# Running two feed-forward units' up halves before their down halves at the start of an attention + MLP kernel

## The chip, the cores and the metric

The kernel runs on one core of a Trainium2 chip. The metric is the device time of one execution, in microseconds; lower is better. Before the change it was 218.37 us, the median of 3 runs (217.48 to 218.43). A run that comes with a profile gives two numbers: its device time, and the span from the first to the last instruction in the trace, which is shorter. The two are never mixed in a subtraction below.

## The reference

Attention over chunks of 32 queries, each with 16 keys to its left, 8 to its right and 8 memory keys, then a normalisation and a two-layer MLP with a residual:

```python
for c in range(S // 32):                    # q, k, v: (4, 8, 768, 64)
    k_full = concat([mem_k, k[:, :, c*32-16 : c*32+40]])     # same for v
    a = softmax(q_c @ k_full.T / 8)
    out[:, :, c*32 : c*32+32] = a @ v_full
x  = out.transpose(0, 2, 1, 3).reshape(4, 768, 512)
xn = (x - mean) / sqrt(var + 1e-6) * g_ln
y  = x + relu(xn @ w_ch1) @ w_ch2           # 512 -> 2048 -> 512
```

## The kernel before

The work is cut into 24 tiles of 128 tokens (6 for each batch entry), and three tiles make a unit, so there are 8 units. Per tile: `scores` (8 matmuls into an `att` slot of PSUM, two exps on ScalarE), `values` (matmuls into the other `att` slot), `norm` (four VectorE instructions that read this slot and leave `xn`), `turn_x` (four transposes of `xn` into a slot, then a ScalarE copy to `xT`). Per unit: 16 `up` chunks (four matmuls of N=384, then a relu on VectorE or ScalarE in turn) and 12 `down` pieces (four matmuls of N=512). PSUM has two `att` slots and four `mm` slots, given out in turn. In the traces every engine takes its instructions in the order of the program; the relu at 40.60 us in the profile after, which stands behind a norm, is the case that matters most.

```python
att = [ps.tile([128, 2, 512], FP32, name=f"att{i}") for i in range(2)]
mm = [ps.tile([128, 512], FP32, name=f"mm{i}") for i in range(4)]
rT = [sb.tile([128, 384], FP16, name=f"rT{hc}") for hc in range(16)]   # one unit's relus
def stay_busy(n, p=None):                  # dummy matmuls on a tile of zeros
    p = slot("mm") if p is None else p
    for _ in range(n):
        nc.tensor.matmul(out=p, lhsT=busy[:, 0:128], rhs=busy, start=True, stop=True)
def clear_q(i, par):                       # zero half of the spread-out queries QZ[i]
    nc.vector.memset(QZ[i][64 - 64 * par : 128 - 64 * par, :, :, par, :], 0.0)
```

The head, cut to TensorE's dummies and VectorE's clears, and the start of unit 0:

```python
stay_busy(10)
clear_v(0, nc.vector, lambda: clear_q(0, 0)); clear_q(0, 1); clear_k(0)
mem_keys(); mem_cols(0)
stay_busy(4)
v_mem(0)                                   # memory rows of the values, by DMA
...                                        # turn keys and queries; stay_busy(3), stay_busy(4)
nc.tensor.matmul(out=banks[2], lhsT=ones32, rhs=g_one, start=True, stop=True)   # g to all rows
nc.vector.tensor_copy(out=g_row, in_=banks[2])
...                                        # tiles 0 to 2: scores, values, norm, turn_x, ups 0-3
for hc in range(4, 8): up(0, 2, hc)
for hc in range(8): up(0, 3, hc, 2)
...                                        # then, in the loop over units, for u == 0:
at(7, clear_q, 1, 0); at(9, clear_q, 1, 1); at(10, clear_k, 1)
at(15, kq_block, ...)                      # second half of batch 0's keys and queries
attend(((17, 19, 19, 22), (18, 21, 21, 24), (20, 23, 23, 26)), "att")   # unit 1's attention
```

`at(step, ...)` places work behind step `step` of a unit: steps 0 to 15 are its ups, the later ones its downs. The numbers of `attend` are the steps of scores, values, norm and turn_x of the three tiles that follow. So before the change, unit 1's attention is spread between unit 0's down pieces.

The softmax here doesn't subtract the row's maximum and nothing guards it: scores larger than these inputs give would overflow.

Of the kernel before, what the change touches and what calls it, by code (L numbers as in the profile page):

```python
# [15 lines left out]
def kernel(  # L16
# [29 lines left out]
    memv16 = sb.tile([72, B, H, HD], FP16, name="memv16")[64:72, :, :, :]  # L46
    memv32 = sb.tile([72, 512], FP32, name="memv32")[64:72, :]
# [12 lines left out]
    qraw = [sb.tile([128, 4096], FP16, name=f"qraw{i}") for i in range(2)]  # L60
    QT = kraw[1]
    k16 = [t[0:96, 0:4096].rearrange("p (h r d) -> p h r d", h=H, r=8) for t in kraw]
    q16 = [t[0:96, 0:4096].rearrange("p (h r d) -> p h r d", h=H, r=8) for t in qraw]
# [7 lines left out]
    rT = [sb.tile([128, 384], FP16, name=f"rT{hc}") for hc in range(16)]  # L71
    osb = [sb.tile([128, 512], FP32, name=f"osb{i}") for i in range(3)]
    total = [sb.tile([128, 1], FP32, name=f"total{i}") for i in range(3)]
    nmean = [sb.tile([128, 1], FP32, name=f"nmean{i}") for i in range(3)]
# [29 lines left out]
    def load_kq(b, which, lo=0, hi=96, h0=0, h1=H):  # L104

        dst, src = ((k16, k), (q16, q))[which]
        nc.gpsimd.dma_start(
            out=dst[b % 2][lo:hi, h0:h1, :, :],
            in_=dram(src, (b * H + h0) * HS + 512 * lo,
                     [[512, hi - lo], [HS, h1 - h0], [1, 512]]),  # L110
        )
# [22 lines left out]
    def v_mem(b):  # L134
        src = memv16[:, b, :, :]
        nc.sync.dma_start(
            out=V[b % 2][96:104, :, :, :],
            in_=bass.AP(tensor=src.tensor, offset=src.offset,
                        ap=[list(src.ap[0]), [0, NG], [1, H * HD]]),
        )  # L140
# [68 lines left out]
    def kq_block(b, j, g0, g1, kind, last=nc.scalar.copy):  # L209

        pk, pq = slot("att"), None
        if kind == "att":
            pq = slot("att")
            pq = [pq[:, i, :] for i in range(2)]
        else:
            pq = [slot("mm")[:, :] for i in range(2)]
        for i in range(2):
            turn_kq(as16(pk[:, i, :]), k16[b % 2], j + i, 96)
        for i in range(2):
            turn_kq(as16(pq[i]), q16[b % 2], j + i, 96)  # L220

        def keep(i):
            keep_k(as16(pk[:, i, :]), b, j + i, 96, g0 + 1 if g0 else 0, g1)
            for par in range(2):
                keep_q(last if i else nc.scalar.copy, as16(pq[i]), b, j + i, par, 96, g0, g1)

        keep(0)
        kept_later.append(lambda: keep(1))
# [11 lines left out]
    def load_tokens(b, which, t):  # L240
        dst, src = ((kraw[0], k), (qraw[0], q))[which]
        nc.gpsimd.dma_start(  # L242
            out=free(dst, 512 * t, [[64, H], [1, 64]]),
            in_=dram(src, b * H * HS + 128 * t * D, [[D, 128], [HS, H], [1, 64]]),
        )
# [7 lines left out]
    def cross_q(half, t0, t1):  # L253
        nc.sync.dma_start_transpose(
            out=free(QT, (24 * half + 4 * t0) * 64, [[64, 4 * (t1 - t0)], [1, 64]]),
            in_=qraw[0][64 * half : 64 * half + 64, 512 * t0 : 512 * t1],
        )
# [58 lines left out]
    def norm(t, xi):  # L316
        x, p = xs[xi], summed.pop(t)
        r, i = rec[t % 2], t % 3
        nc.vector.reciprocal(out=r, in_=free(p, 64, [[128, H]]))
        nc.vector.scalar_tensor_tensor(  # L320
            out=x.rearrange("p (h d) -> p h d", h=H),
            in0=free(p, 0, [[128, H], [1, 64]]), scalar=1.0,
            in1=free(r, 0, [[1, H], [0, 64]]),
            op0=ALU.mult, op1=ALU.mult, accum_out=total[i],
        )
        nc.vector.tensor_scalar(  # L326
            out=nmean[i], in0=total[i], scalar1=-1.0 / 512, scalar2=None, op0=ALU.mult,
        )
        nc.vector.scalar_tensor_tensor(  # L329
            out=xn[i], in0=x, scalar=nmean[i], in1=g_row, op0=ALU.add, op1=ALU.mult,  # L330
        )

    def root(t, xi):
        i = t % 3
        nc.scalar.activation(  # L335
            out=junk, in_=xs[xi], func=ACTF.Square, bias=nmean[i], accum_out=squares[i],
        )
        nc.gpsimd.tensor_scalar(  # L338
            out=veps[i], in0=squares[i], scalar1=1.0 / 512, scalar2=1e-6,
            op0=ALU.mult, op1=ALU.add,  # L340
        )
        nc.gpsimd.tensor_tensor(out=rstd[xi], in0=veps[i], in1=mhalf, op=ALU.pow)  # L342
# [27 lines left out]
    def up(u, n, hc, t0=0, on_act=False):  # L370
# [10 lines left out]
        o = rT[hc][:, lo:hi]  # L381
# [7 lines left out]
    def down(t, i, part):  # L389
# [3 lines left out]
        for hc in range(4 * part, 4 * part + 4):  # L393
            nc.tensor.matmul(  # L394
                out=p, lhsT=rT[hc][:, 128 * i : 128 * i + 128],
                rhs=w2c[hc // 4][:, hc % 4, :],
                start=(hc == 0), stop=(hc == 15),
            )
# [7 lines left out]
    def down_last(t, i):  # L406

        o = osb[t % 3]
        for lo, hi in ((0, 256), (256, 384), (384, 512)):
            p = slot("mm")[:, 0 : hi - lo]  # L410
            for hc in range(16):
                nc.tensor.matmul(  # L412
                    out=p, lhsT=rT[hc][:, 128 * i : 128 * i + 128],
                    rhs=w2c[hc // 4][:, hc % 4, lo:hi],
                    start=(hc == 0), stop=(hc == 15),
                )
# [17 lines left out]
    def clear_q(i, par):  # L434

        nc.vector.memset(QZ[i][64 - 64 * par : 128 - 64 * par, :, :, par, :], 0.0)  # L436

    def clear_v(i, eng, between=lambda: None):
# [3 lines left out]
        eng.memset(V[i][:, :, :, 64:HD], 1.0)  # L442
        between()
        for c, g in enumerate((0, NG - 1)):
            eng.tensor_copy(
                out=free(V[i][:, g, 0, 64:65], 0, [[HD, H]]),
                in_=free(counts[:, c : c + 1], 0, [[0, H]]),
            )
# [14 lines left out]
    nc.vector.memset(memv16[:, :, :, 64:HD], 1.0)  # L463
# [3 lines left out]
    for h in (0, 4):  # L467
        for which in range(2):
            load_kq(0, which, 0, CUT[which], h, h + 4)
    keep(counts[:, 0:1], counts[:, 0:1], 16, 0.0)  # L470
    keep(counts[:, 1:2], counts[:, 1:2], -80, 0.0)
    make_identity(nc, identity)
    nc.scalar.copy(out=memk16, in_=memk32)
    nc.scalar.copy(out=memv16[:, 0, :, 0:64], in_=memv32.rearrange("p (h d) -> p h d", h=H))
    stay_busy(10)
    clear_v(0, nc.vector, lambda: clear_q(0, 0))
    clear_q(0, 1)
    clear_k(0)
    mem_keys()
    mem_cols(0)  # L480
    stay_busy(4)
    v_mem(0)
    for g in range(6):
        load_v_group(0, g)
# [11 lines left out]
    for c in range(4):  # L496
        load_w1(c)
    for which in range(2):
        load_kq(0, which, CUT[which], 96)
    load_w2(0)  # L500
    load_w2(1)
    for g in range(6, 10):
        load_v_group(0, g)
    load_w2(2)
    for g in range(10, NG):
        load_v_group(0, g)
    load_w2(3)
# [10 lines left out]
    spare = att[(turn["att"] + 1) % 2][:, 0, :]  # L518
    for j in range(2):
        turn_kq(first_k[j], k16[0], j, CUT[0])  # L520
    for j in range(2):
        turn_kq(first_q[j], q16[0], j, CUT[1])
# [5 lines left out]
    for j in range(2, 4):  # L528
        turn_kq(first_k[j], k16[0], j, CUT[0])
# [3 lines left out]
    for j in range(2, 4):  # L533
        turn_kq(first_q[j], q16[0], j, CUT[1])
# [4 lines left out]
    nc.tensor.matmul(out=banks[2], lhsT=ones32, rhs=g_one, start=True, stop=True)  # L539
    nc.vector.tensor_copy(out=g_row, in_=banks[2])  # L540
# [22 lines left out]
    turn_x(0, 2, 2)  # L563
    for hc in range(4, 8):
        up(0, 2, hc)
    for hc in range(8):
        up(0, 3, hc, 2)
# [3 lines left out]
    for u, tiles in enumerate(units):  # L571
        n = len(tiles)
        following = units[u + 1] if u + 1 < len(units) else []
        plan = {}

# [3 lines left out]
        def attend(steps, kind="dma"):  # L579

            for i, (s0, s1, s2, s3) in enumerate(steps):
# [5 lines left out]
                at(min(s3 + 3, 27), root, t % 6, t % 9)  # L587
# [10 lines left out]

        if u == 0:
            at(7, clear_q, 1, 0)  # L600
            at(9, clear_q, 1, 1)
            at(10, clear_k, 1)
            at(23, clear_v, 1, nc.gpsimd)
            for j in (0, 2):
                at(15, kq_block, 0, j, 6, NG, "mm", nc.vector.tensor_copy if j else nc.scalar.copy)
                at(15, keep_rest)
            for t in range(3):
                at(19 + t, root, t, t)
            for h in (0, 4):
                for which in range(2):  # L610
                    at(15, load_kq, 1, which, 0, 96, h, h + 4)
            for g in range(6):
                at(23, load_v_group, 1, g)
            attend(((17, 19, 19, 22), (18, 21, 21, 24), (20, 23, 23, 26)), "att")
            at(26, mem_cols, 1)
            at(26, v_mem, 1)
        elif u == 1:
            for j in (0, 2):
                at(5 + 3 * j, kq_block, 1, j, 0, NG, "att")
                at(7 + 3 * j, keep_rest)  # L620
            for g in range(6, NG):
                at(0, load_v_group, 1, g)
            for t in range(6):
                for which in range(2):
                    at(14, load_tokens, 2, which, t)
            attend(((16, 19, 19, 22), (17, 19, 20, 23), (21, 23, 23, 26)), "att")
# [34 lines left out]
        for step in range(16 + 4 * n):  # L661
            if step < 16:
                if u or step > 7:
                    up(u, n, step)
            else:
                i, part = divmod(step - 16, 4)
                if u == 0:
                    i, part = (step - 16) % 3, (step - 16) // 3
                if following or i < n - 1:
                    down(tiles[i], i, part)  # L670
# [34 lines left out]
```

## Time and profile before

| | before |
|---|---|
| device time, median | 218.37 us |
| span of the profiled run | 216.0 us |
| TensorE busy | 210.2 us, 97% |
| VectorE / ScalarE busy | 118.6 / 99.7 us |
| VectorE stall of TensorE behind the head | one, 0.71 us at 28.44 us |

TensorE is the bound. The page of the profile adds one line that becomes important later: the clock that TensorE was granted, in 40 equal slices of the span, each digit in tenths of full speed.

```profile
PEclk9999999999999999999999999999999999999998
```

Two quantities are used in what follows. The first is the *lost time* of a TensorE instruction: the time from its predecessor's start to its own start, less the time that the predecessor takes in steady state (0.216 us for N=512, 0.1625 for N=384, 0.056 for N=128, all from unbroken stretches of this trace). It doesn't depend on the modelled ends of matmuls. The second is the start of the first exp, which marks the end of the head: 13.07 us before.

### The profile page before, as it was taken

Reading aid. Unit: us, or ns where it says so; the run is one execution under the profiler, and the core shown is the slowest. Engines: PE = TensorE matmul, PEld = TensorE weight load, DVE = VectorE, ACT = ScalarE, POOL = GpSimd, SP = SyncE. Lnnn points to the kernel's source line nnn. Section 1 sums busy time; section 2 is a strip of 40 time slices with the busy share of each in tenths; the row PEclk is TensorE's granted clock in tenths of the full one; section 3 lists DMA queues with packets and bytes.
Section 4 is the critical chain, followed back from the end, with each engine's and each line's share of the span. In section 5 each row is a group of like instructions: output and inputs, shape, how many; then the busy total and the mean of one; then the engine's idle time right before and its main releaser. Section 6 shows DMA issues by size and latency. Waiting matters only on the chain.

```text
span 216.0 us, 5059 instructions
## 1 busy us (share of the span) xinstructions
PE 210.2 (97%) x2011; PEld 129.8 (60%) x2011; DVE 118.6 (55%) x274; ACT 99.7 (46%) x206; POOL 104.4 (48%) x185
## 2 busy tenths in 40 slices
PE   7999989999999999999999999999999999999993
PEld 2557866557765577546754676456754675466562
DVE  6967675685737548524375349224484447634222
ACT  4478437855893677302653167103761275314100
POOL 7993245699996318974004998507145000400000
PEclk9999999999999999999999999999999999999998
DMA  5999999999999989996312999997674101330012
GB/s 78 182 150 207 209 208 181 200 206 226 148 140 172 102 135 146 151 146 171 48 27 80 142 186 148 138 156 103 176 150 132 49 3 24 91 108 0 0 49 100
DMA packets 87714, 27.37 MB, mean 127 GB/s; under 512 B 78297, under 2 KB 84185, under 8 KB 87642
## 3 DMA queue, kind: packets, MB, share of 16 engines
q0 software_dynamic: 62128, 14.38, 78.2%
q1 hardware_dynamic: 25562, 12.66, 28.2%
q8 instruction: 16, 0.26, 0.5%
q14 instruction: 8, 0.07, 0.1%
HBM read 28.84 MB, written 6.29 MB: 163 GB/s over the span
## 4 chain that ended last, share of the span: by engine, by line
PE 94%; DVE 3%; ACT 1%; issue 1%; ACTq 0%
PE mm L377 37%; PE mm L394 37%; PE att L289 5%; PE att L309 3%; PE mm L366 3%; PE att L179 2%; PE mm L412 2%; PE mm L179 1%; DVE QZ L436 1%; ACT AT L296 1%; PE att L352 1%; PE att L366 1%; DVE rT L385 1%; PE mm L539 0%; DVE xn L329 0%
## 5 line engine op out<-in xcount | busy, mean ns | idle before, releaser
L377 PE MATMUL mm<-xT,w1c 128*128 128x384 f16 (+2 forms) x560 | 89.0, 313 | 0.6 <-DVE rT L385 0.6
L394 PE MATMUL mm<-w2c,rT 128*128 128x512 f16 x368 | 84.4, 379 | 0.0
L377 PEld LDWEIGHTS <-w1c 128*128 128x128 f16 x560 | 58.8, 114 | 23.6 <-issue 1.0
L383 ACT ACTIVATE rT<-mm 128x384 f16<-128x384 f32 (+2 forms) x74 | 33.1, 453 | 72.4 <-PE mm L377 50.2
L394 PEld LDWEIGHTS <-rT 128*128 128x128 f16 x368 | 34.7, 98 | 37.5
L385 DVE TENSOR_SCALAR rT<-mm 128x384 f16<-128x384 f32 (+2 forms) x66 | 34.9, 533 | 33.6 <-PE mm L377 33.5
L401 DVE SCALAR_TENSOR_TENSOR osb<-mm,rstd,xs 128x512 f32<-128x512 f32 x23 | 17.3, 750 | 41.8 <-PE mm L394 24.9
L296 ACT ACTIVATE AT<-att,band 104x512 f16<-104x512 f32 x48 | 30.2, 683 | 9.6 <-PE att L289 8.2
L338 POOL TENSOR_SCALAR veps<-squares 128x1 f32<-128x1 f32 x24 | 4.8, 200 | 42.7 <-ACT junk L335 41.3
L117 POOL DMA_DIRECT2D V<-in_v_dram x24 | 18.4, 772 | 11.0 <-DMA w1c<-in_moe_w_ch_dram 7.8
L335 ACT ACTIVATE junk<-xs,nmean 128x512 f16<-128x512 f32 x24 | 17.3, 721 | 7.1 <-DVE nmean L326 6.7
L329 DVE SCALAR_TENSOR_TENSOR xn<-xs,nmean,g_row 128x512 f16<-128x512 f32 x24 | 18.8, 782 | 0.9
L320 DVE SCALAR_TENSOR_TENSOR xs<-att,rec 128x512 f32<-128x512 f32 x24 | 16.6, 691 | 0.8
L289 PEld LDWEIGHTS <-KT 128*128 128x128 f16 x192 | 12.6, 98 | 4.6 <-issue 1.0
L277 POOL COPY QZ<-kraw 64x768 f16<-64x768 f16 x16 | 13.2, 826 | 3.9 <-DMA kraw<-qraw 3.4
L342 POOL TENSOR_TENSOR rstd<-veps,mhalf 128x1 f32<-128x1 f32 x24 | 13.7, 571 | 2.0
L289 PE MATMUL att<-QZ,KT 128*128 128x128 f16 x192 | 14.6, 219 | 0.0
L269 POOL COPY KT<-KT 128x128 f16<-128x128 f16 (+4 forms) x16 | 4.2, 292 | 18.2 <-DMA KT<-kraw 18.1
L123 POOL DMA_DIRECT2D V<-in_v_dram x16 | 12.0, 791 | 0.9 <-PE mm L377 0.7
L309 PEld LDWEIGHTS <-AT 104*64 104x64 f16 x384 | 7.5, 111 | 6.5 <-ACT AT L296 2.1
L242 POOL DMA_DIRECT2D qraw<-in_q_dram x12 | 11.3, 938 | 0.0
L242 POOL DMA_DIRECT2D kraw<-in_k_dram x12 | 11.2, 934 | 0.0
(76 smaller groups left out, 136.6 us busy)
## 6 DMA issues: line engine op xcount, KB each, us to landing
out_dram<-osb SPq DMA_DIRECT2D x23, 256.0 KB, 2.3
V<-in_v_dram POOLq DMA_DIRECT2D x36, 96.0 KB, 6.9
w1c<-in_moe_w_ch_dram POOLq DMA_DIRECT2D x4, 512.0 KB, 9.6
w2c<-in_moe_w_ch_dram POOLq DMA_DIRECT2D x4, 512.0 KB, 13.5
kraw<-in_k_dram POOLq DMA_DIRECT2D x12, 128.0 KB, 5.3
qraw<-in_q_dram POOLq DMA_DIRECT2D x12, 128.0 KB, 5.4
qraw<-in_q_dram POOLq DMA_DIRECT2D x3, 384.0 KB, 11.6
kraw<-in_k_dram POOLq DMA_DIRECT2D x3, 256.0 KB, 5.7
```

What stands on the lines that cost most here:

```text
L117: nc.gpsimd.dma_start(out=V[b % 2][r : r + hi - lo, g, :, 0:64], in_=dram(v, b * H * HS + lo * D, [[64, hi - lo], [HS, H], [1, 64]]),)
L242: nc.gpsimd.dma_start(out=free(dst, 512 * t, [[64, H], [1, 64]]), in_=dram(src, b * H * HS + 128 * t * D, [[D, 128], [HS, H], [1, 64]]),)
L289: nc.tensor.matmul(out=p[:, gg, 128 * j : 128 * j + 128], lhsT=KT[b % 2][:, (4 * g + j) * KW : (4 * g + j) * KW + 128], rhs=QZ[b % 2][:, g ...
L296: nc.scalar.activation(out=free(a, 32 * c, [[512, 2], [64, 8], [1, 32]], KR), in_=free(p, 32 * c, [[512, 2], [64, 8], [1, 32]], KR), func= ...
L320: nc.vector.scalar_tensor_tensor(out=x.rearrange("p (h d) -> p h d", h=H), in0=free(p, 0, [[128, H], [1, 64]]), scalar=1.0, in1=free(r, 0, ...
L329: nc.vector.scalar_tensor_tensor(out=xn[i], in0=x, scalar=nmean[i], in1=g_row, op0=ALU.add, op1=ALU.mult,)
L335: nc.scalar.activation(out=junk, in_=xs[xi], func=ACTF.Square, bias=nmean[i], accum_out=squares[i],)
L377: nc.tensor.matmul(out=p, lhsT=free(w, i, [[4, 128]]), rhs=xT[u % 2][:, dt, lo:hi], start=(dt == 0), stop=(dt == 3),)
L383: nc.scalar.activation(out=o, in_=p, func=ACTF.Relu)
L385: nc.vector.tensor_scalar(out=o, in0=p, scalar1=0.0, scalar2=None, op0=ALU.max)
L394: nc.tensor.matmul(out=p, lhsT=rT[hc][:, 128 * i : 128 * i + 128], rhs=w2c[hc // 4][:, hc % 4, :], start=(hc == 0), stop=(hc == 15),)
L401: nc.vector.scalar_tensor_tensor(out=o, in0=p, scalar=rstd[t % 9], in1=xs[t % 9], op0=ALU.mult, op1=ALU.add,)
```

## The change

As far as the diff shows, the intent is to start unit 0's and unit 1's ups together, both before any down, so that w2 isn't needed so early and the loads can come in order of use; and to take work off VectorE and the DMA queues in the head. The core of the diff, with cuts marked:

```diff
-rT = [sb.tile([128, 384], ...) for hc in range(16)]
+rT = [[... 16 tiles for even use ...], [kraw[1][:, 384*hc : 384*hc+384] for hc in range(10)] + [... 6 tiles]]
+def keep_mem(b, g0, g1):                   # memory rows of V by a VectorE copy, not DMA
+    nc.vector.tensor_copy(out=V[b % 2][96:104, g0:g1, :, 0:64], in_=<memv16, repeated>)
-def clear_q(i, par):
+def clear_q(i, par, g0=0, g1=NG):          # half clears
...
-stay_busy(10)
-clear_v(0, nc.vector, lambda: clear_q(0, 0))
-clear_q(0, 1)
-clear_k(0)
+nc.scalar.copy(out=QZ[0][0:64, 0:6, :, 1, :], in_=<zeros>)   # this part of the clear is now ScalarE's
+stay_busy(8)
+clear_v(0, nc.vector, lambda: (clear_q(0, 0, 0, 6), clear_k(0)), 33)   # ones as 32-bit words
 mem_keys()
+spare = att[turn["att"]]
+nc.tensor.matmul(out=spare[:, 1, :], lhsT=ones32, rhs=g_one, ...)      # broadcast of g, earlier
+nc.scalar.copy(out=g_row, in_=spare[:, 1, :])
 mem_cols(0)
-stay_busy(4)
-v_mem(0)
...                                         # loads: w1 quarter by quarter between k, q, v; w2 last
-nc.tensor.matmul(out=banks[2], lhsT=ones32, rhs=g_one, ...)
-nc.vector.tensor_copy(out=g_row, in_=banks[2])
+keep_mem(0, 0, 6)
...
 turn_x(0, 2, 2)
-for hc in range(4, 8): up(0, 2, hc)
-for hc in range(8): up(0, 3, hc, 2)
+for hc in range(4): up(0, 3, hc, 2)
+for par in range(2): clear_q(0, par, 6, NG)
+keep_mem(0, 6, NG)
+stay_busy(2)
+for j in (0, 2): kq_block(0, j, 6, NG, "mm", vec if j else act); keep_rest()
+for hc in range(4, 7): up(0, 3, hc)
+scores(0, 3); up 7; scores(0, 4); up 8, 9; values(0, 3); norm(3, 3); up 10
+values(0, 4); norm(4, 4); up 11; scores(0, 5)
+turn_x(1, 0, 3); up(1, 1, 0..3); values(0, 5); norm(5, 5); turn_x(1, 1, 4)
+up(1, 1, 4..7); up(1, 2, 0..7, 1); up(1, 2, 8..11); turn_x(1, 2, 5)
+up(0, 3, 12..15); up(1, 3, 0..11, 2)
...
+down_tiles = units[0] + units[1] if u == 1 else tiles     # 24 downs in one row
-for j in (0, 2): at(5 + 3 * j, kq_block, 1, j, 0, NG, "att")
+for j in (0, 2): at(21 + 2 * j, kq_block, 1, j, 0, NG, "att")   # batch 1 turned in unit 0's down
-attend(((16, 19, 19, 22), (17, 19, 20, 23), (21, 23, 23, 26)), "att")
+attend(((30, 32, 32, 35), (30, 33, 33, 36), (34, 36, 36, 39)), "att")
```

In calls such as `up(1, 2, hc, 1)` the numbers are: unit, end of the row tiles, chunk, first row tile. So `up(1, 1, hc)` does one row tile only, four matmuls of N=128.

## The prediction

> **What bounds the kernel now.** I began with the page's busy shares, then took the busy time by stretches, which says where TensorE is not already working:
>
> ```profile
> PE 210.2 (97%) x2011; PEld 129.8 (60%) x2011; DVE 118.6 (55%) x274; ACT 99.7 (46%) x206; POOL 104.4 (48%) x185
> ```
>
> ```profile
> 0.00:18.30 18.30, 16.65 (x242) 8.36 (x243) 14.19 (x40) 10.23 (x20) 14.88 (x36) 1.00 1.56 145
> 18.30:24.60 6.30, 6.28 (x93) 5.90 (x90) 3.84 (x11) 4.40 (x15) 2.15 (x3) 1.00 1.24 206
> 24.60:29.30 4.70, 4.16 (x29) 2.81 (x27) 3.98 (x7) 1.85 (x5) 1.72 (x3) 1.00 1.18 214
> 29.30:47.40 18.10, 18.09 (x269) 11.09 (x269) 11.96 (x34) 11.80 (x25) 11.93 (x21) 1.00 1.41 196
> 47.40:74.80 27.40, 27.40 (x326) 17.64 (x325) 17.07 (x39) 18.52 (x34) 21.98 (x33) 1.00 1.88 164
> 74.80:212.40 137.60, 137.57 (x1065) 83.96 (x1062) 67.22 (x145) 52.94 (x110) 51.78 (x92) 1.00 0.81 103
> ```
>
> The second column is the stretch, the third TensorE's busy time. From 29.3 us TensorE is never idle. Busy alone proves little, since ends are modelled, so I checked the pace in the chain of waits:
>
> ```profile
> 24.66 0.29 DVE rT L385
> 24.95 0.38 issue
> 25.32 1.34 DVE QZ L436
> 26.66 0.03 issue
> 26.69 0.56 DVE rT L385
> 27.25 0.26 issue
> 27.51 1.34 DVE QZ L436
> 28.85 0.42 DVE rT L385
> ...
> 33.62 1.83 PE mm L394 x8
> ...
> 87.86 10.36 PE mm L394 x48
> 98.22 6.50 PE mm L377 x40
> ```
>
> 48 down matmuls in 10.36 us are 0.216 us each, 40 up matmuls in 6.50 are 0.1625. It runs at its own rate. Only one stall lies behind the head: two VectorE memsets of 1.34 us between relus hold the four PSUM slots until 29.31 (TensorE's last start before was 28.44, so about 0.7 us are lost). Before 18.3 TensorE waits under dummy matmuls, on loads, VectorE copies and the first softmax. So the change can win only there: perhaps 1 us of head and 0.7 of stall. All useful matmuls remain. What it can lose is open-ended, since unit 0's ups no longer have long downs between them and a tile's attention.
>
> **What the Trainium skill says.** "VectorE: DVE Perf Modes", section "Zero memsets can be issued as uint32 (trn2)": a memset costs per element, whatever the type. The trace agrees in kind: 1536 elements take 1.34 us as uint32 (QZ) and 1.34 as f16 (ones of V). So halving QZ's clear and writing only 96 32-bit words of ones should shorten them to about 0.7 and 0.15 us. The same page, "The perf-mode tier table", gives a 16-bit SBUF-to-SBUF copy four elements a cycle. The trace has one, mem_cols: 384 elements in 0.26 us, while 8-element copies take 0.18. If 0.17 is fixed, the rest fits four a cycle. My estimate for half of the value mem rows (6 groups x 8 heads x 64 = 3072) is 0.17 + 3072/4/0.96 ns = 0.97 us. "TensorE: Matmul & The Clock Gate", "Back-to-back issue gap": N/2.4 + 2.5 ns, 0.216 us for 512; the 0.216 above agrees.
>
> **The change, part by part.** Durations that I use, of single instructions in the timeline before: a norm on VectorE 1.92 us (16.78 to 18.69: reciprocal, product 0.69, scaling 0.15, 0.75), its PSUM input read after 0.95; relu 0.56 (N=384) or 0.29 (N=128) on VectorE; exp pair 1.26; xT copy 0.585; batch 0's second-half copies out of PSUM 3.5 us of VectorE (31.62 to 35.32).
>
> ```profile
> 16.19 1.26 ACT L296 ACTIVATE AT<-att,band 104x512 f16<-104x512 f32 x2 [0.70 <-PE att L289]
> 17.36 0.58 ACT L357 COPY xT<-mm 128x512 f16<-128x512 f16 x1
> ...
> 19.76 0.75 DVE L329 SCALAR_TENSOR_TENSOR xn<-xs,nmean,g_row 128x512 f16<-128x512 f32 x1
> ```
>
> *Head.* VectorE sheds about 3.7 us of memsets (0.48 memv, 1.2 ones of V, 2.0 QZ) and the 0.69 us g_row copy, and the fp32 broadcast (1.05 us just ahead of the first scores) moves into the start, in place of dummies. But first-half loads and the unchanged dummies still hold the last q turn near 10.6 (10.68 before). Scores then follow its copies rather than the broadcast, and exp starts at about 12.4 instead of 13.07. Copying the mem rows follows on VectorE until about 13.75, so values(0,0) starts at 13.8, not 14.39: **-0.55**. The stall at 28.4 goes: **-0.7**. DMA should gain slack: the 120 KB mem-row transfer leaves the head and w2 comes last. At some 2.5 us per weight quarter (the trace's landings: 17.8, 20.3, 22.9) I have w1's parts down by 15.7, 20.6, 24.4 and 29.5, ahead of every use. It ends no wait.
>
> *From xn of tile 2 on*, by hand, in engine order, shifted by -0.5:
> - turn_x(0,2) is now followed by ups that need its very copy; before, ups of tiles 0 and 1 stood there. Latency 0.25 + copy 0.58: **+0.8**. Two new dummies after it: 2 x 0.216 = **+0.4**.
> - Four N=128 ups end near 22.4. VectorE then does two half clears (0.7 each, 0.3 gap ahead of each as before) and the second mem copy (0.97), until 25.7; the kq copies take 3.5 more, until 29.2. TensorE turns both blocks (2.75 us) and does three ups (1.95) by 27.8, then waits for QZ of the last pair: **+1.3**.
> - scores(3) about 29.2, values(3) ends 32.35. Norm 3 is 32.57 to 34.5, the relu of up 10 is behind it, and norm 4 has read its PSUM only at 35.95. turn_x(1,0) needs that slot (the att ring has two), and TensorE has run out of other work at 34.75: **+1.2**. Then the xT copy ahead of up(1,1,0): **+0.85**.
> - up(1,1,4)'s relu is behind norm 5 on VectorE. After values(5), 1.2 us of TensorE work fill the four slots; the relu comes 2.5 us after it: **+1.25**.
> - N=128 pieces: 4 x 55.8 against 4 x 54.2 ns for a third of a chunk; 12 chunks against 4 in three pieces: **+0.2**.
>
> That puts unit 1's loop at about 50 us. The trace before gives the same work done at 61.1 (end of unit 1's up) less unit 0's down 10.35, batch 1's turns 3.3 and four ups 2.6, that is 44.9. Check: 50 - 44.9 = 5.1, against 6.0 - 1.25 + small gaps from the list.
> - Turning batch 1 within downs (steps 21 and 25): its first keys' copy gets behind two clears, a V clear and an output on VectorE, so the second block waits a little for its slot: **+0.5** (0 to 1).
> - The last turn_x stands at the last step, 39, with no down behind it (before: step 26 of 27); unit 2's first up waits for the copy: **+0.9**.
>
> Sum: losses 7.4, gains 1.25, net +6.15. 218.4 + 6.1 = **224.5 us**. Loop steps of 0.86 us cover the rest (scores to values two steps, V and tokens landing before their use).
>
> **Rivals.**
> 1. *The stalls are less, time unchanged (217 to 220).* The head might gain more, if the VectorE clears truly held it; for that speaks VectorE's 14.2 busy us of 18.3. Against: q's second half lands at 9.46 whatever VectorE does. Or the copies' order leaves ups to fill the holes; against that, engines take instructions in order. The author probably laid these positions out on the chip, which is why I keep 0.3 for "same".
> 2. *The mem copy is slow or loses its turn to GpSimd.* At two a cycle 1.7 us, with the head's gain gone and the second hole 0.7 longer: 226. Its kin took 0.40 at 47.2 against 0.26 at 8.7, beside GpSimd's DMA issuing.
> 3. *The start becomes DMA-bound.* If V or the kq rest land late: 227 or more. DMA was full to 50 us before, but the order of the loads now follows the order of use.
> 4. *Faster by 1.* Only if both gains stay and no hole opens: 217.
>
> **Range and chances.** The holes at turn_x, the slot and the relu behind norm 5 (4.1 us together) are hard dependences; the rest may shrink by half or double. Range 219.5 to 227.5. Slower by over 2% needs over 222.7, 1.8 below my number: 0.66. Faster by 2% needs 4.4 us where 1.25 are to be had: 0.02.
>
> **What would show it.** Right: in the chain VectorE and ScalarE pieces between 20 and 42 us that sum to 5 or more; TensorE's first turn_x of unit 1 released by norm 4's product; up(1,2,0) released by a relu; a gap ahead of unit 2's first up released by an xT copy; the first mem copy 0.9 to 1.1 us; nothing waiting on w1 or w2; busy TensorE throughout from unit 2 on. Wrong: scores starting before 11 us, TensorE packed from 21 to 45, or a DMA landing ending a TensorE wait.

## The result, and the profile after

The changed kernel took 225.6 us (median of 4 runs, 224.59 to 227.94), the kernel before 218.11 in the same rounds (4 runs, 217.48 to 218.43). The ratio is 1.036, with a 95% interval of 1.027 to 1.045: slower. Ratios here are the mean time of one kernel's fast runs over that of the other's of the same rounds, so they aren't quite the ratio of the medians that are quoted. The result lies in the predicted range, 1.1 us above the predicted number.

The page after. The first line is the span, the second the busy times, the third the granted clock:

```profile
span 222.9 us, 5194 instructions
PE 211.5 (95%) x2071; PEld 132.1 (59%) x2071; DVE 120.6 (54%) x285; ACT 103.2 (46%) x216; POOL 104.5 (47%) x185
PEclk9699999999999999999999999999999999999999
```

TensorE is busy 1.3 us more than before, and the span is 6.9 us longer. So most of the loss is idle time. The busy time by stretches of the changed kernel says where (second column the length, third TensorE's busy time, then weight loads, VectorE, ScalarE, GpSimd, the granted clock and the DMA columns):

```profile
0.00:21.20 21.20, 19.00 (x277) 10.85 (x278) 13.38 (x43) 14.37 (x31) 17.37 (x38) 0.92 1.22 151
21.20:42.00 20.80, 16.54 (x313) 13.16 (x311) 15.27 (x40) 12.10 (x29) 8.95 (x16) 1.00 1.38 199
42.00:52.70 10.70, 10.70 (x116) 9.10 (x115) 5.83 (x15) 5.84 (x17) 0.00 (x0) 1.00 0.77 127
```

From 21.2 to 42 us TensorE is idle for 4.3 us; from 42 to 52.7 us it is packed again, and the waits behind that are in the table below. Note the 0.92 in the first line, which the kernel before doesn't have. The chain of waits of the changed kernel, in order of time, names who held TensorE (start, length, engine, tile, line, number of instructions):

```profile
21.40 0.59 ACT xT L367
...
22.04 1.06 PE mm L387 x16
23.09 0.43 PE mm L376 x2
...
25.02 0.73 DVE V L146
...
28.87 0.57 DVE QZ L214
...
29.48 0.44 PE att L299 x5
...
35.34 0.71 DVE xs L330 x2
...
36.09 0.40 PE att L362 x4
...
36.51 0.60 ACT xT L367
...
37.15 1.05 PE mm L387 x16
...
40.60 0.21 DVE kraw L395
...
40.85 3.73 PE mm L387 x48
```

Read it hole by hole, a hole being a wait of TensorE. At 21.4 TensorE waits for ScalarE's copy of xT of tile 2 (L367), then come the two dummies (L376). At 28.87 it waits for VectorE's copy of queries (QZ, L214), which is late behind the second memory copy (V, L146) and the copies of keys. At 35.34 it waits for the product of norm 4 (xs, L330), which reads the PSUM slot that turn_x needs, and then at 36.51 for the xT copy. At 40.60 it waits for a relu (`kraw` is where unit 1's relus now lie, L395), which stands in the timeline straight behind norm 5's last instruction (39.85 to 40.60). All five were named in the prediction.

| Lost TensorE time | predicted | measured |
|---|---|---|
| first exp earlier | -0.55 | 0.0 |
| stall at 28.4 removed | -0.7 | -0.71 |
| xT copy of tile 2 | +0.8 | 0.84 |
| two dummies | +0.4 | 0.43 |
| QZ of the last pair | +1.3 | 0.99 |
| `att` slot behind norm 4 | +1.2 | 1.19 |
| xT copy ahead of up(1,1,0) | +0.85 | 0.84 |
| relu behind norm 5 | +1.25 | 1.22 |
| N=128 pieces | +0.2 | not separable |
| batch 1's second block, 62.6 us | +0.5 | 0.64 |
| unit 2's first up, 80.4 us | +0.9 | 0.84 |
| wait for V's rows, 162 us | none | 0.59 |
| sum | +6.15 | 6.87 |

The measured terms are from one trace; differences under 0.2 us aren't listed. Their sum agrees with the difference of the two spans, 222.9 - 216.0 = 6.9. So the profile accounts for the result. But it leaves four things to settle: whether these holes add up independently, where the head's gain went, why the changed kernel spreads by 3.4 us from run to run when the kernel before spreads by 1, and what the order would be worth with its holes filled.

### The profile page after: what moved, and what is told of

It is laid out like the page before. It is cut to its first block, busy times and chain, and to the rows that moved or that the text cites. A ratio compares the mean times of both kernels' runs of the same rounds, so it can differ in the third digit from the quotient of the medians.

```text
span 222.9 us, 5194 instructions
## 1 busy us (share of the span) xinstructions
PE 211.5 (95%) x2071; PEld 132.1 (59%) x2071; DVE 120.6 (54%) x285; ACT 103.2 (46%) x216; POOL 104.5 (47%) x185
## 4 chain that ended last, share of the span: by engine, by line
PE 77%; DMA 9%; DVE 8%; SPq 2%; issue 2%; ACT 1%; POOL 1%; DVEq 0%; POOLq 0%
PE mm L404 31%; PE mm L387 31%; DMA V<-V 4%; PE att L299 4%; PE att L319 3%; DMA KT<-kraw 3%; PE att L189 2%; DMA qraw<-in_q_dram 2%; DVE xs L330 2%; PE mm L422 2%; DVE KT L204 1%; DVE xn L339 1%; PE att L376 1%; PE mm L189 1%; DVE QZ L214 1%
## 5 line engine op out<-in xcount | busy, mean ns | idle before, releaser
L387 PE MATMUL mm<-xT,w1c 128*128 128x384 f16 (+2 forms) x624 | 90.1, 298 | 3.2 <-ACT xT L367 2.0
L404 PE MATMUL mm<-w2c,rT 128*128 128x512 f16 x338 | 76.3, 379 | 0.0
L387 PEld LDWEIGHTS <-w1c 128*128 128x128 f16 x624 | 60.6, 114 | 24.4 <-issue 2.6
L393 ACT ACTIVATE rT<-mm 128x384 f16<-128x384 f32 (+2 forms) x68 | 30.7, 455 | 71.4 <-PE mm L387 49.3
L404 PEld LDWEIGHTS <-rT 128*128 128x128 f16 x338 | 32.4, 98 | 36.9
L395 DVE TENSOR_SCALAR rT<-mm 128x384 f16<-128x384 f32 (+2 forms) x60 | 32.2, 540 | 36.4 <-PE mm L387 36.4
L330 DVE SCALAR_TENSOR_TENSOR xs<-att,rec 128x512 f32<-128x512 f32 x24 | 16.6, 691 | 0.8
L287 POOL COPY QZ<-kraw 64x768 f16<-64x768 f16 x16 | 14.0, 874 | 3.8 <-DMA kraw<-qraw 3.2
```

What stands on the lines that cost most here:

```text
L330: nc.vector.scalar_tensor_tensor(out=x.rearrange("p (h d) -> p h d", h=H), in0=free(p, 0, [[128, H], [1, 64]]), scalar=1.0, in1=free(r, 0, ...
L387: nc.tensor.matmul(out=p, lhsT=free(w, i, [[4, 128]]), rhs=xT[u % 2][:, dt, lo:hi], start=(dt == 0), stop=(dt == 3),)
L393: nc.scalar.activation(out=o, in_=p, func=ACTF.Relu)
L395: nc.vector.tensor_scalar(out=o, in0=p, scalar1=0.0, scalar2=None, op0=ALU.max)
L404: nc.tensor.matmul(out=p, lhsT=rT[t // 3 == 1][hc][:, 128 * i : 128 * i + 128], rhs=w2c[hc // 4][:, hc % 4, :], start=(hc == 0), stop=(hc ...
```

## The experiments

My theory was that each hole is a hard dependence of the new order and that the holes add up. The first rival was that some of them are one wait under two names; the second that the loss and the spread come from the clock and not from the order. All runs below gave correct results. A run of one look has one time only, with an unknown state, so I use its trace and not its time. "First exp" is its start in the trace; where it moves, everything behind it moves.

### r_after: the changed kernel once more

No edit. 3 rounds.

> The changed kernel unaltered, to see how far its own runs differ. Theory (holes): the five waits of TensorE between 20 and 42 us (xT copy 0.84, QZ of the last pair 0.99, slot behind norm 4 1.19, xT copy 0.84, relu behind norm 5 1.22), the one at unit 2's first up (0.84) and the one in batch 1's turning (0.64) return within 0.1 us each, because they hang on instruction order; ratio to before 1.03 to 1.04. Rival (DMA or clock noise makes the loss): those waits change from run to run and the spread of 224.6 to 227.9 us comes from them.

Measured: 227.3 us (4 runs, 226.22 to 228.91) against 217.89 (7 runs), ratio 1.045 (1.039 to 1.052), just above the 1.03 to 1.04 that I expected. That is 1.7 us above the first result. The holes have the same sizes (0.836, 0.995, 1.196, 0.835, 1.224, 0.648, 0.836 us), yet all of them lie later, and the first exp is at 14.98, not 13.08. So the holes are not what varies. The reason can be read off the dummies of the head, which do the same work in each run. The group of four dummies in the kernel before (start, duration):

```profile
9.72 1.04 PE L366 MATMUL att<-busy 128*128 128x512 f16 x4
```

In the first profile of the changed kernel:

```profile
9.71 1.54 PE L376 MATMUL att<-busy 128*128 128x512 f16 x4
```

And in this run:

```profile
11.25 1.89 PE L376 MATMUL att<-busy 128*128 128x512 f16 x4
```

They start 0.43 us apart here and 0.216 apart before: half the rate. The clock records agree. Before, the clock is full from 6.67 us on. In the first profile of the changed kernel it was full from 3.93, half again from 7.34 to 10.76 (the 6 in the page's clock line), and then full to the end; in this run it was full only from 13.04. The mean clock of this run, 0.999, hides it, because the time before the first record counts as full. The Trainium skill describes the mechanism, in "TensorE: Matmul & The Clock Gate", section "Part 1: The HAM clock gate": the clock is halved by default, about 3.4 us of sustained activity release it, and the window is free-running, so that the transition differs between runs. The records here last 3.41 us or multiples of it, which agrees.

### e_slot: turn_x(1, 0) in another slot

```diff
-    turn_x(1, 0, 3)
+    turn_x(1, 0, 3, "mm")
```

> Only the first turn of unit 1 takes one of the four single-bank PSUM slots in place of one of the two attention slots. As the prediction counts it, the slot costs 1.2 us and the copy after it another 0.85: then TensorE gains 1.2 us. Rival: ScalarE's exp of tile 5 is ahead of that copy in its queue and ends at 36.4 us anyway, so the transposes start at once (about 34.9) but the first up of unit 1 still starts at about 37.05 instead of 37.14, and the gain is 0.1 us.

Measured: 225.81 us, one look. The transposes now follow the scores at once, at 36.21, and the product of norm 4 holds nothing. But the next up waits for longer:

```profile
36.46 1.27 ACT L306 ACTIVATE AT<-att,band 104x512 f16<-104x512 f32 x2
37.62 0.59 ACT L367 COPY xT<-mm 128x512 f16<-128x512 f16 x1
...
38.25 0.44 PE L387 MATMUL mm<-xT,w1c 128*128 128x128 f16 x5 [1.66 <-ACT xT L367]
```

The lines are of this run's timeline; the bracket is the idle time and what ended it. ScalarE takes the exp pair of tile 5 first, and the xT copy only at 37.62. The lost time is 1.82 us in one piece, against 1.19 + 0.84 = 2.03 in two: 0.2 us won. So the rival is right for this pair. The slot and the copy are not two independent costs of 2 us; behind the slot stands a path of nearly the same length, by way of ScalarE.

This trace shows one thing more. Behind the hole the clock was half once again, well after the head (the stretches of its windows; the column behind GpSimd's busy time is the granted clock):

```profile
39.76:43.17 3.41, 3.34 (x33) 3.07 (x32) 2.47 (x8) 1.34 (x4) 0.11 (x1) 0.50 1.22 196
43.17:46.60 3.43, 3.43 (x45) 3.32 (x44) 1.72 (x5) 1.67 (x7) 0.00 (x0) 1.00 1.24 205
```

The ups of N=128 start 0.107 us apart in the first of these stretches and 0.056 apart behind it. (So "for good at 15.9 us", which the expectation of e_warm says of this run, isn't right.) No other profile here has a half clock between the head and the last matmuls, and whether the hole brought it isn't shown; but the clock can be lost behind the head too.

### e_act: relus of up(1, 1, 4..7) on ScalarE

```diff
     for hc in range(4, 8):
-        up(1, 1, hc)
+        up(1, 1, hc, 0, True)
```

> Only the relus of unit 1's chunks 4 to 7 of the first row tile all go to ScalarE, so none stands behind norm 5 on VectorE. If the wait of 1.22 us ahead of the up at 40.85 us is that relu, it shrinks to 0.5 or less (the next relu on VectorE comes four ups later) and everything after it comes 0.7 to 1.1 us earlier. Rival (the slot ring is full for another reason): the wait stays over 1 us.

Measured: 228.43 us, one look, with the clock full only from 20.25 us and the first exp at 15.59, so the time says nothing. In the trace the wait behind norm 5 is down from 1.22 to 0.21 us, with 0.12 us more in the ups just ahead of it, and TensorE then runs on. The hole was the order on VectorE, as predicted.

### e_fill: ups of unit 0 put into the holes

```diff
     scores(0, 5)
+    up(0, 3, 12); up(0, 3, 13)
     turn_x(1, 0, 3)
+    up(0, 3, 14); up(0, 3, 15)
...                                  # turn_x(1, 2, 5) to ahead of up(1, 2, 8..11)
-    for hc in range(12, 16):
-        up(0, 3, hc)
```

> Only the order of work: unit 0's last four ups (2.6 us, w1's last quarter landed at 32.7) are put around the first turn of unit 1, two ahead of it and two behind it. If the two waits there (1.19 and 0.84 us) are only lack of other work, both fall under 0.15 us and the start of unit 1's loop comes 1.9 us earlier; the relu wait behind norm 5 stays near 1.2. Rival: the relus of the moved ups stand behind norm 4 on VectorE and make a new wait of 0.5 us or more at the first ups of unit 1; gain 1.4 us or less.

Measured: 223.76 us, one look; first exp at 13.55, 0.5 later than in the profile after. Both waits are gone, and the relu wait, which I hadn't touched, is as it was:

```profile
36.92 0.39 PE L362 MATMUL att<-identity,xn 128*128 128x128 f16 x4
37.14 2.42 PE L387 MATMUL mm<-xT,w1c 128*128 128x384 f16 x24
...
42.23 1.98 PE L387 MATMUL mm<-xT,w1c 128*128 128x128 f16 x32 [1.07 <-DVE kraw L395]
```

The transposes carry no bracket, and ups of N=384 run straight behind them while ScalarE copies. The matmul ahead of the relu wait starts at 40.94, 1.36 us later than in the profile after; 0.7 of that is the later head (the wait for QZ lies at 29.14, not 28.44), and four more chunks (2.6 us) are already done by then. So 2.6 - 1.36 + 0.7 = 1.94 us are won, which is nearly the 2.03 of the two holes together. What the slot alone doesn't give back, other work does; no run takes away the copy alone.

### e_keeps: the clears earlier, the memory copy later

```diff
+    for par in range(2): clear_q(0, par, 6, NG)    # in the head, after the first keep_k loop
...
-    for par in range(2): clear_q(0, par, 6, NG)
-    keep_mem(0, 6, NG)
-    stay_busy(2)
...
     for hc in range(4, 7): up(0, 3, hc)
+    keep_mem(0, 6, NG)
```

> VectorE's half clears of QZ move into its idle stretch of the head, the second mem copy behind the three ups, and the two new dummies ahead of batch 0's turning go. If the wait for QZ of the last pair (0.99 us at 28.44) comes of VectorE being late with 2.8 us of other work, it falls under 0.3 us, and the distance from turn_x of tile 2 to the end of scores(3) shrinks from 8.4 to 7.0 us. Rival (the keys' and queries' copies alone, 3.5 us, are the bound): the wait stays near 1 us and only the dummies' 0.43 us are won.

Measured: 224.52 us, one look. The wait for QZ (0.985) and the dummies (0.43) are gone. From turn_x(0, 2) to turn_x(1, 0) it takes 35.11 - 21.41 = 13.70 us; in the profile after it takes 36.09 - 20.98 = 15.11. So 1.41 us are won, of the 1.4 that the two terms hold.

### e_last: the last turn_x of unit 2 a step earlier

```diff
-            attend(((30, 32, 32, 35), (30, 33, 33, 36), (34, 36, 36, 39)), "att")
+            attend(((30, 32, 32, 35), (30, 33, 33, 36), (33, 35, 35, 38)), "att")
```

> Batch 1's third tile goes one step earlier, so its last turn stands at step 38 and one down (0.86 us) lies behind it. If the 0.84 us ahead of unit 2's first up is that copy's latency, it falls under 0.1 us. Rival (the norm of that tile, or PSUM slots, come later anyway): the wait only moves to the turn itself, 0.4 us or more ahead of it.

Measured: 225.75 us, one look, clock full for good only from 18.41 us. The wait of 0.84 us ahead of unit 2's first up is gone: a down piece of 1.03 us now stands over the copy. The term was right.

### e_warm: four dummies put back after mem_cols

```diff
     mem_cols(0)
+    stay_busy(4, spare)
```

> Four dummy matmuls come back behind the broadcast in the head, nothing else. Theory (clock gate): in the traces of the changed kernel so far the full clock was granted for good only at 10.8, 13.0, 15.9, 20.3 and 11.2 us (before: 6.7), and the start of unit 1's loop is late by as much as the head; with dummies as many as before full clock comes at about 7 and stays, first exp starts at 12.5 to 13.1 us in the profile, the runs lie within 1 us of each other, median 223.5 to 224.5 us. Rival (the spread is of the DMA or another): median and spread stay at 225 to 228 us.

Measured: 230.49 us (4 runs, 224.73 to 232.17), but three runs, and the profiled one among them, are slow; the one fast run took 224.73. The trace is of a slow run and can't be compared with the fast ones, but it shows that the edit isn't a clean test: the dummies write the tile from which ScalarE copies g_row, and TensorE waited 0.67 us for that copy. In that run the clock was full only from 19.58 us and the first exp was at 18.13.

### e_warm2: the dummies back, the broadcast later

```diff
-stay_busy(8)
+stay_busy(10)
...
 mem_cols(0)
+stay_busy(4)
...
-stay_busy(4, spare)
+nc.tensor.matmul(out=g_all, lhsT=ones32, rhs=g_one, ...)   # g_all in the att slot beside spare
...
 keep_mem(0, 0, 6)
+nc.vector.tensor_copy(out=g_row, in_=g_all)
```

> The same question in another form: ten dummies, the mem keys and four dummies as before the change, and the fp32 broadcast moved behind the second turn of keys in place of the four dummies there. If the broadcast (one row of the array) doesn't count as activity for the clock gate, this one holds the full clock from 6.7 us where the other may not: first exp at 12.4 to 13.0, median 223.5 to 224.5, spread under 1 us. Rival: no difference to the changed kernel.

Measured: 227.99 us (4 runs, 227.15 to 228.44), ratio 1.047 (1.043 to 1.051). This failed too: the second scores needed the `att` slot that held the broadcast, and TensorE stood idle for 3.23 us until VectorE had copied it. The clock, full from 4.36 us, was half again from 11.19 to 18.01. So it isn't a test of the clock alone. Nor does it show that the idle time brought the half clock, which began only about 0.5 us after TensorE's last matmul ahead of that wait.

### e_warm3: the head's TensorE order of before

```diff
-stay_busy(8)
+stay_busy(10)
...                                  # the early broadcast and the ScalarE copy of g_row removed
 mem_cols(0)
+stay_busy(4)
...                                  # after the last turn of queries, as before the change
+nc.tensor.matmul(out=banks[2], lhsT=ones32, rhs=g_one, start=True, stop=True)
 keep_mem(0, 0, 6)
+nc.vector.tensor_copy(out=g_row, in_=banks[2])
```

> The changed kernel with the head's TensorE order of before: ten dummies, mem keys, four dummies, the broadcast behind the last turn of queries and its copy on VectorE (the two earlier tries brought waits of their own). Theory (clock gate): full clock at 6.7 to 8 us and kept, first exp at 13.0 to 13.3 us as before, every run within 1 us of 224.6 (the holes alone: profile span 222.5 to 223.5). Rival: spread of 3 us and more as in the changed kernel.

Measured: 225.16 us (4 runs, 224.62 to 225.54) against 218.46 (11 runs, 217.36 to 219.30), ratio 1.032 (1.027 to 1.037). The dummies run at full rate:

```profile
9.53 1.04 PE L376 MATMUL att<-busy 128*128 128x512 f16 x4
```

The clock is full from 6.28 us to the end, the first exp is at 12.88, and the runs spread by 0.9 us, where the changed kernel's eight runs spread by 4.3. All the holes are there in full (0.84, 0.98, 1.19, 0.84, 1.23, 0.65, 0.84), and the wait near 162 us is 0.98. So with the head's order as before, the order of the units costs 6.7 us in medians; and this points to the head, and not to the order of the units, as what makes the changed kernel's time vary. It is no more than a pointer: the eight runs are of other rounds, four of them at least on another chip, and the other three runs of e_warm3 list mean clocks of 0.984 to 0.997, so they too had some half clock.

### b_cold: the kernel before with fewer dummies

```diff
-    stay_busy(10)
+    stay_busy(8)
...
     mem_cols(0)
-    stay_busy(4)
```

> The kernel before with six of its fourteen first dummies away (8 and 0, as in the change), nothing else. Theory (clock gate): TensorE's full clock comes later or is lost again in the head, first exp after 13.5 us in the profile, runs spread over 2 us or more, median 218.5 to 222. Rival (the dummies only fill waits on the loads): 217.5 to 218.5 as before, no spread.

Measured: 221.84 us (4 runs, 221.10 to 222.46) against the same 218.46, ratio 1.016 (1.012 to 1.021), so 3.4 us by medians. In the profiled run the clock was full only from 20.40 us, and the dummies that are left ran at half the rate, as in r_after (1.04 us for these four in the kernel before):

```profile
10.28 1.89 PE L366 MATMUL att<-busy 128*128 128x512 f16 x4
```

Without the six dummies the first turn of keys even starts earlier (5.71 us, before 7.22), but the first exp is at 16.20, 3.1 us later. The shift came; the spread that I had expected, of 2 us or more, did not (1.4, where the kernel before itself spread by 1.9 in these rounds). So six dummies that do no useful work are worth 3.4 us by medians, and the clock is the reason that the trace shows. Not all of this profile's longer span is the clock, though: 0.78 us more are lost ahead of a transpose at 38.51 us, and nothing in the trace says why.

### e_all3: e_warm3 with all four repairs

The edits of e_fill, e_act, e_keeps and e_last on top of e_warm3; the half clears stand right after mem_cols.

> The changed kernel with the head's TensorE order of before and all four repairs of holes (relus on ScalarE, four ups moved, half clears in the head and no new dummies, last turn a step earlier). By the holes that each took away: 224.6 - 0.9 - 1.95 - 1.4 - 0.84 = 219.5, ratio to before 1.005 to 1.01; left are the xT copy behind the turn of tile 2 (0.84), batch 1's turning (0.65) and a DMA wait near 161 us (0.5 to 1.1). If something else in the two-unit order costs, it stays above 221; if the order itself is a gain that the holes hid, it is under 217.5.

Measured: 219.88 us (4 runs, 218.98 to 220.65), ratio 1.007 (1.003 to 1.012). That is 5.3 us below e_warm3. Those holes gave back nearly all that they had cost, and the order is still no faster than the kernel before. What is left in the profiled run is new, four waits for quarters of w1 (0.77, 0.32, 0.24 and 0.99 us), of which the timeline names two:

```profile
18.75 0.86 PE L387 MATMUL mm<-xT,w1c 128*128 128x128 f16 x12 [0.60 <-DMA w1c<-in_moe_w_ch_dram]
...
35.31 1.01 PE L387 MATMUL mm<-xT,w1c 128*128 128x384 f16 x5 [0.83 <-DMA w1c<-in_moe_w_ch_dram]
```

In this run the four quarters landed at 18.70, 26.44, 30.21 and 35.27 us, in the profile after at 17.28, 23.05, 26.88 and 32.66. With the earlier landings none of the four waits would be there. The runs don't show why the landings were later here; the profiled run is also the slowest of the four. The wait near 162 us, 0.98 us in e_warm3, is absent, so not all of the 5.3 us need come from the four repairs.

### b_clear: the kernel before without its one stall

```diff
-            at(7, clear_q, 1, 0)
-            at(9, clear_q, 1, 1)
+            at(16, clear_q, 1, 0)
+            at(17, clear_q, 1, 1)
```

> The kernel before with batch 1's two QZ clears (1.34 us each on VectorE) moved from unit 0's ups to its first two down steps, where VectorE waits 3.2 us. The only wait of TensorE behind the head, 0.71 us at 28.4, should go: 217.1 to 217.5, ratio 0.996 to 0.998. Rival (the next VectorE work, norm 3, is then late): same time as before, with a wait near 38 us.

Measured, in 5 rounds: 217.44 us (6 runs, 217.09 to 218.04) against 218.46, ratio 0.996 (0.993 to 0.9995). Within the 2% that counts as the same; the interval lies just below 1. But the runs' mean clocks suggest that most of this isn't the edit's doing. Of the eleven runs of the kernel before, the five with 0.997 or more took 217.36 to 217.62 us (mean 217.47), and the six with 0.991 to 0.996 took 218.46 to 219.30. The six of b_clear all have 0.998 or more, and their mean is 217.46. So among runs of like mean clock no gain in device time is shown. The chain of waits between 21 and 33 us, where VectorE's memsets stood before:

```profile
21.46 8.73 PE mm L377 x80
30.20 0.80 PE att L179 x32
```

The two clears now lie beside unit 0's first downs, when VectorE has no relus that free slots. The stall of 0.71 us is gone; a wait of 0.61 us for the first quarter of w1 at 17.79 us in the profiled run is not of this edit's making, since the quarter landed at 18.38 there and at 17.82 before. No wait near 38 us came in its place. So the stall behind the head goes by moving two lines, even if the device time doesn't show what that is worth.

## Why the prediction was right or wrong

**What bounds it: right.** TensorE was packed from 29.3 us on before, so a new order could only win in the head and at one stall. The stall went, as predicted, and b_clear's trace shows that it goes without the new order too. Whether its 0.7 us reach the device time isn't shown: 0.7 is less than the 1.9 us by which the kernel before differs from run to run in the same rounds.

**The holes behind tile 2: right, by name and nearly by size.** Eight of the terms were foreseen, and seven of them came within 0.15 us; QZ of the last pair was 0.3 us less than predicted. e_fill, e_act, e_keeps and e_last each remove the holes that they aim at, and e_all3 removes 5.3 us by doing all of it. So these causes are shown and not only argued. The copy of tile 2 (0.84) and batch 1's second block (0.64) are read from traces alone; no run takes them away.

**"turn_x(1,0) needs that slot: +1.2. Then the xT copy: +0.85": the sum right, the separation wrong.** The prediction treats them as two costs. e_slot shows that without the slot wait the copy is 1.82 us late, because the exps of tile 5 stand ahead of it on ScalarE. In a sum of waits, each term holds only as long as the other engines' order stays as it is.

**"Exp starts at about 12.4 instead of 13.07: -0.55": the mechanism right, the gain lost to the clock.** The first exp was at 13.08, and values(0, 0) at 14.45 instead of the predicted 13.8. That scores would follow the copies and no longer the broadcast did come: the first exp starts 1.90 us behind the last turn of queries (11.18 to 13.08), where it was 2.39 before (10.68 to 13.07), so 0.49 are won there. The step that failed is "the unchanged dummies still hold the last q turn near 10.6". They start as before (9.71, before 9.72), but run for most of their length at half the clock, so that the last turn starts at 11.18, 0.50 later, and the gain is gone. In r_after it starts at 13.07, again 1.91 ahead of the first exp. Behind this is "in place of dummies", which took the dummies for filling: the change leaves 8 of the first 14, and b_cold shows that this alone costs the kernel before its full clock. In the changed kernel the early broadcast stands in the same stretch, and no run separates the two. Whether the early broadcast wins its half microsecond when the clock is full isn't shown: e_warm and e_warm2 brought waits of their own, and e_warm3 puts the broadcast back, so its first exp at 12.88 is no test of it.

**The range: right, for a reason that it didn't name.** I gave 219.5 to 227.5 for holes that might halve or double. The holes hardly varied; the clock did. The two medians of the changed kernel, 225.6 and 227.3, lie 1.7 us apart, and its first exp in the two profiles 1.9. With the head of before the median is 225.16. The second median lies 0.2 below the upper edge, and three of the eight runs lie above it, so that the result came within 1.1 us of the number is in part luck.

**The loads: no wait in the changed kernel, but mis-sized.** The prediction has w1's quarters down by 15.7, 20.6, 24.4 and 29.5 us; they landed at 17.28, 23.05, 26.88 and 32.66, 1.6 to 3.2 us later. The holes hid this. (Its "DMA was full to 50 us before" is short too: the DMA row of the page before is at eight tenths or more to about 100 us.)

**Not foreseen: the wait near 162 us.** A DMA landing that ends a TensorE wait is one of the prediction's own signs of being wrong, and here it came. There a later tile's values wait for the DMA that moves V's neighbour rows, by 0.59 us here and 0.98 in e_warm3. In the chain of the changed kernel:

```profile
153.45 9.12 DMA V<-V
...
162.70 0.70 PE att L319 x30
```

It lands 9.1 us after its issue; before, it took 7.0 (147.00 to 153.99). Its cause stays open: no run changes what precedes it alone, and it is absent in e_all3 and in e_slot.

**Rivals.** The second (the memory copy slow) is out for most runs: the first copy took 0.96 or 0.97 us in eight of the eleven profiles of the new order, where the estimate was 0.97. But it took 1.32 in r_after, 1.23 in e_fill and 1.32 in e_last, and in the first two the first values waited 0.26 and 0.17 us for it. The third (bound by DMA) didn't happen in the changed kernel, where nothing waited for w1 or w2; it shows in e_all3, once the holes are filled. The first and the fourth (no loss, or a gain) are refuted by every timed run of the order except e_all3, which needs four repairs and the old head to come within 0.7%.

## What to carry to other kernels

Where the bound engine is packed, a reordering wins nothing except at the waits that exist, and it has to be checked dependence by dependence in engine order: work that used to stand over a copy, a slot or a relu is what is lost when it is moved. Dummy matmuls in a head may be holding the clock; look at the granted clock and at the pace of equal matmuls before removing any, and repeat the run, since one profile can show a luckier head than the next. And try the smallest edit for the known stall first: here moving two lines took it out of the trace, and the large change lost 3.6%. Before a small gain is believed, compare runs of like clock: b_clear's 0.4% does not outlast that.

## What the Trainium skill lacked or had wrong

- "TensorE: Matmul & The Clock Gate", section "Part 1: The HAM clock gate", agrees with the 3.41 us steps of the clock here. It puts the price of the ramp at under 1% of a typical span. In b_cold, six dummies fewer cost 1.6% (3.4 us of 218), and the clock was not full before 20.40 us, although TensorE was busy for 18.5 of the first 20.4 us. What a one-row fp32 matmul or a run of short transposes counts for as activity isn't told beyond a remark, in "Part 4: PE-mode transpose", that transposes don't count the same way; no run here separates the two.
- The same page, section "Back-to-back issue gap", gives a sustained rate of about 131 ns for N=512 beside the formula for the isolated gap. The 48 down matmuls of the kernel before ran at 216 ns each, in a sustained stream with a weight load for each: the formula holds and the sustained figure doesn't.
- "VectorE: DVE Perf Modes", section "Zero memsets can be issued as uint32 (trn2)", says one cycle per element; at the 0.96 GHz of the same page 1536 elements would take 1.60 us. They took 1.34, and 768 took 0.70.
- I found no page that says that the mean granted clock of a profile counts the time before its first record as full: 0.999 was given for a run whose clock was full only from 13.04 us.
